# The dense layer's low halves on VectorE instead of GpSimd, in an attention and mixture-of-experts kernel on one core

## The chip, the core and the metric

The kernel runs on one core of a Trainium2 chip. A core has TensorE (matrix products, written PE in the profile, its weight loads PEld), VectorE (DVE), ScalarE (ACT), GpSimd (POOL) and SyncE (SP, which issues DMAs). The metric is the time of one execution on the device in microseconds (us).

## What is computed

The reference has three parts, each feeding the next. Shapes are those of the run.

```python
# q, k, v: (4, 8, 576, 64); attention in blocks of 64 rows, lower-triangular by blocks
attn = softmax(mask(q @ k.T / sqrt(64)));  x = attn @ v        # -> 2304 tokens x 512
# dense layer (the "moe" of the reference)
h = x @ w_in              # 512 -> 2048, float64 weights
g = h - tanh(h)
x = g @ w_out             # 2048 -> 512
# routed layer: 8 experts, top 1, tokens with x @ w_skip <= 0 pass through
e = argmax(x @ w_gate); p = max(softmax(x @ w_gate))
y = x + p * (relu(x @ w1[e]) @ w2[e])
```

## The kernel before

All products run on float32r operands in pairs: a value is split into a high half `hi`, a rounded copy that ScalarE makes, and a low half `lo = value - hi`, and a product is the sum of three matmuls, hi·lo, lo·hi and hi·hi. So each operand that is made on the chip costs one copy on ScalarE and one subtraction on another engine.

The order of every engine's work is the order in which the program is written; nothing is rescheduled. After the attention comes the dense layer, `moe1`. It takes the hidden axis in two halves of 1024. In each half it walks over six groups of 384 tokens, and in each group over eight chunks of 128 hidden values: 96 steps in all, numbered s, 48 in the first half and 48 in the second. A step does this:

- `hidden(s)` (L508): 12 matmuls of 384 columns, into one of three PSUM banks `h`.
- `mm2(s-3)` (L561): 9 matmuls of 512 columns that add the chunk of three steps ago to three PSUM banks `acc`, one for each 128 tokens.
- `act(s)`: g = h - tanh(h) with a polynomial in place of tanh for small h. ScalarE makes u (L533), t (L534) and y (L535), VectorE makes w from h and u (L536), t = h - t (L537), w from y and w (L538). Then `split_g(s-1)` splits the previous step's w into `gh` (ScalarE, L549) and `gl` (L550). Then ScalarE makes the mask k (L541), and VectorE puts t into w where k says so (L542). t, u, y and k have one buffer each, so L534 of the next step waits for L542 of this one.
- `X.split` (L448, L449), in four of each group's eight steps: a quarter of the next group's tokens, `xg`, is split into the pair `xhl`, the high half on ScalarE and the low half in L449.
- `side(s)`: in the first half a decoder turns the float64 weights into pairs. One chunk takes ScalarE's L48, VectorE's L49 to L52, and then ScalarE's L53 and GpSimd's subtraction L54, the last two in the step after. 20 chunks are spread over the 48 steps: one in every second step of the first eight, then two in every five.

When a group's eight steps are summed, `finish` runs from inside `act`, ahead of L541. In the first half it copies the three banks `acc` on ScalarE (L578) and stores them. In the second half VectorE adds the first half's sums (L584), and the rows go through the routing: TensorE turns them (L602, with one PSUM bank for it), ScalarE and VectorE split them (L608, L609), then come logits and small VectorE operations, and GpSimd scatters the records with indirect DMAs (L685).

The routed layer follows: GpSimd gathers tokens (L801), and TensorE runs L834 and L893.

Of the kernel before, what the change touches and what calls it, by code (L numbers as in the profile page):

```python
# [9 lines left out]
F32 = mybir.dt.float32  # L10
# [21 lines left out]
class Decoder:  # L32
    """float64 words -> hi/lo float32r pairs, one chunk of 512 values per partition at a time."""

# [28 lines left out]

class Plan:
    """The order in which the query blocks of a pair of heads go through the attention, and how many
    blocks each stage runs behind the scores."""

# [10 lines left out]
class Banks:  # L78
    """The eight banks of PSUM, three of them for each of two uses and two single ones."""

# [12 lines left out]
def attention(nc, tc, ctx, d, ident, q, k, v, xTd, PS, spare, between, ending, NP=None):  # L93
    """spare: 6144 float32r a partition, used up to the last pair but one"""
    L = ctx.enter_context(tc.tile_pool(name="attl", bufs=2))
# [5 lines left out]
    pt0 = P.tile([128, 2, 4, 128], F32, name="pt0")  # L101
    # blocks 4-8 of the probabilities: four chunks of keys each, and the last block's fifth behind three of zeros
    pts = []
# [51 lines left out]
    def prep_q(n, bank=PS.single):  # L155
        """transposes of q into the two diagonal blocks, scaled"""
        qr, qb = raws[n][1], qbd[n % 2]
        pq, pr = bank(), bank()
        for j in range(4):
            nc.tensor.transpose(pq[:, 128 * j:128 * j + 128], qr[:, j].rearrange("p h d -> p (h d)"), ident)  # L160
        nc.tensor.transpose(pr[:, 0:64], qr[0:64, 4].rearrange("p h d -> p (h d)"), ident[0:64, 0:64])
        yield
        for hh in range(2):
            sl = slice(64 * hh, 64 * hh + 64)
            evac_q(qb[sl, 0:8, sl], pq[sl].rearrange("d (i n) -> d i n", i=8))
            evac_q(qb[sl, NB - 1, sl], pr[sl, 0:64])
        yield
# [76 lines left out]
    def transposes(n, i):  # L244
        """emits the transposes of block i; notes the copies out of PSUM that they allow"""
        nj = i // 2 + 1
# [39 lines left out]
    def pv_early(n):  # L286
        """blocks 0-3 of both heads"""
        vr = vrs.pop(n)
        xp = PS.single()
        for hh in range(2):  # L290
            hs = slice(64 * hh, 64 * hh + 64)
            for j in range(2):
                nc.tensor.matmul(
                    xp[hs, 128 * j:256].rearrange("p (i c) -> p i c", c=64), vr[:, j, hh, :],
                    pt0[:, j, 2 * j:4, hs], start=(j == 0), stop=(j == 1),
                )
        yield
        xs = L.tile([128, 256], F32, tag="xs0", name="xs0", bufs=2)
        evac("xs0", xs, xp[:, 0:256])
        yield  # L300
        b, hp = pairs[n]
        nc.sync.dma_start(out=xTd[hp * 128:hp * 128 + 128, b * d.S:b * d.S + 256], in_=xs)

    def pv_late(n, hh, xs):
        """blocks 4-8 of one head"""
        vv = vhl[n % 2]
# [23 lines left out]
    load(1)  # L330
    # the tensor engine's clock rises while the first rows are on their way
    w = PS("acc")
# [55 lines left out]
NSLOT, MORE = 256, 128  # L388
# the units of routed tokens after the first expert's two: where the ones of MORE tokens stand among those of NSLOT
UNITS = (NSLOT, NSLOT, MORE, NSLOT, MORE, NSLOT, MORE)  # L390
# [5 lines left out]
class Route:  # L396
    """Tables of the routed tokens by expert.

    The first unit is filled by the expert that leads after NEARLY groups, with tokens of all
    groups but the last; the last group's tokens of that expert follow in its next units."""  # L400

# [23 lines left out]
class Tokens:  # L425
    """The attention's rows, transposed, as hi/lo pairs of a group at a time; loaded for each half."""

# [15 lines left out]

    def split(self, u, c, eng=None):
        if u >= 2 * NG:
            return
        xg, x = self.raw.pop((u, c)), self.hl[u]
        self.nc.scalar.copy(x[:, 0, c], xg)  # L448
        (eng or self.nc.gpsimd).tensor_tensor(x[:, 1, c], xg, x[:, 0, c].bitcast(F32), op=ALU.subtract)  # L449


class Consts:
    def __init__(self, nc, pool, d):
# [30 lines left out]
        self.col = index("col", [e, e], [[0, e], [1, e]])  # L484
        # the experts before each one
        self.before = t([128, e, e], F32, name="before")
# [12 lines left out]
def hidden(nc, X, PS, W, hs, s):  # L499
    """chunk s % 8 of a half's hidden axis, for a group of tokens"""  # L500
    u, f = divmod(s, 8)
# [11 lines left out]
def moe1(nc, tc, ctx, X, T, PS, d, C, W, x2p, x2s, tab, out, side, route, hs):  # L513
    """g(x w_in) w_out in two halves of the hidden axis; the second half routes the tokens.

    W[h] = (w_in, w_out) as [128, 2, 4, 1024] and [128, 2, 8, 512] hi/lo pairs.
    side(step) runs other work between the chunks. Returns the last group's routing, to be
    advanced by the caller."""
    P = ctx.enter_context(tc.tile_pool(name="m1", bufs=1))
# [25 lines left out]
    def split_g(s):  # L545
# [3 lines left out]
        nc.scalar.copy(gh, w)  # L549
        nc.gpsimd.tensor_tensor(gl, w, gh.bitcast(F32), op=ALU.subtract)  # L550

# [18 lines left out]
    def finish(u):  # L570
        """the token tiles of a group, once their sums are complete"""
        g = u % NG
# [17 lines left out]
        lp = PS("lp")  # L590
        # in the weights of w_out that are not in use: the other half's, and then this one's
        xh, xl = (
# [60 lines left out]
        nc.scalar.activation(ex, ex, AF.Exp)  # L653
        # the active ones as a factor of the one-hot rows; then what moves the others out of the table
        nc.vector.scalar_tensor_tensor(v, v, 1.0, b8(m2), op0=ALU.mult, op1=ALU.is_equal)
# [96 lines left out]
class Moe2:  # L752
    """The experts' two products over units of 256 or 128 routed tokens."""

# [6 lines left out]
    def load_piece(self, e, j, q=None):  # L761
        """piece j (of 8) of an expert's weights, as it lies in memory; e may be a register"""
        nc = self.nc
# [64 lines left out]
    def mm1(self, x, w, f):  # L828
        """the hidden layer's chunk f, transposed"""
        wi, h = self.W[w][0], self.PS("h")  # L830
# [9 lines left out]
    def mm1_few(self, x, w, z):  # L840
        """chunks 2z and 2z + 1 of the hidden layer of MORE tokens, as rows of tokens"""
        wi, h = self.W[w][0], self.PS("h")
# [76 lines left out]
    def prepare(self, row):  # L919
        """the first unit's tokens, as steps"""  # L920
        self.recs, self.xrs, self.xx = {0: self.load_rec(row, self.nc.sync)}, {}, {}
# [9 lines left out]
    def run(self, sizes, lead, tail, then, units):  # L931
        """units of sizes[k] tokens; the first two are the leading expert's, whose weights are in place.

        tail: the last group's routing, and then() what follows it; units(): (expert, first record)
        of the units from the third on"""
        K = len(sizes)
# [69 lines left out]
    def one(self, e, row):  # L1006
        """a run of MORE tokens on its own"""
        rec = self.load_rec(row, nt=1)
# [21 lines left out]
def entries(nc, pool, d, C, route, out):  # L1030
    """what remains after the leading expert's two units: (expert, first record row) of each entry, and their number.

    The first entries, up to NBIG, are pairs of MORE tokens (the last of a pair may be short), the
    others are runs of up to MORE tokens; entries past the number are empty ones. As steps."""
    E, N = d.E, NENTRY
# [14 lines left out]
    yield  # L1050
    # the pairs, as many as there are big units; the rest in single runs
    v.tensor_tensor(up, up2(pair), C.before, op=ALU.mult)
# [7 lines left out]
    v.memset(st[:, 2 * E:], float(E * d.NT))  # L1060
    # how many entries end with each expert's
    for z in range(2):
# [14 lines left out]
    yield  # L1077
    # the first row: the expert's first one, and so many tokens as the entries of its kind before hold
    v.tensor_tensor(dif, st[:, 1:], st[:, 0:2 * E], op=ALU.subtract)
# [16 lines left out]
def tile_kernel(ctx, tc, q, k, v, moe_w_in, moe_w_out, moe2_w_skip, moe2_w_gate, moe2_w1, moe2_w2, out):  # L1096
# [44 lines left out]
    def decode(z):  # L1141
        """a chunk of the float64 weights: steps, with loads running two chunks ahead"""
        for i in range(2 if z == 0 else 0):
# [7 lines left out]
    with ExitStack() as actx:  # L1151
# [5 lines left out]
        def between(n):  # L1157
# [12 lines left out]
            if n == 3:  # L1170
                # the rows that the first gather covers and no token has filled by then
                zr = ip.tile([128, 1, d.DM], F32, name="zr")
# [9 lines left out]
        def ending(n):  # L1182
            if FIRST_X <= n < FIRST_X + 2:
                X.split(0, 2 * (n - FIRST_X), nc.vector)
                X.split(0, 2 * (n - FIRST_X) + 1, nc.vector)
            if n == -6:
# [101 lines left out]
```

## Time and profile before

| | |
|---|---|
| median of three runs | 906.24 us (905.58 to 907.66) |
| profiled execution, its span | 904.2 us |
| TensorE busy | 845.3 us (93%) |
| VectorE busy | 732.1 us (81%), 1541 instructions |
| ScalarE busy | 567.2 us (63%) |
| GpSimd busy | 404.5 us (45%), 454 instructions |
| chain that ended last | TensorE 38%, VectorE 30%, "issue" 16%, DMA 5%, ScalarE 5%, GpSimd 3% |
| L550 on GpSimd | 96 times, 1029 ns each |
| L449 on GpSimd | 44 times, 1309 ns each |

The profile is of one execution. Busy time of TensorE includes matmuls that overlap, so a busy TensorE is not one at its peak. The chain is followed back from the last instruction to what released each step. "Idle before, releaser" is the time for which an engine stood still and the instruction that ended it.

### The profile page before, as it was taken

The page shows a single profiled execution, that of the slowest core. Times are in us where ns is not written, and L with a number is a line of the kernel's source. Part 1 is how long each engine was busy: PE and PEld are TensorE (multiplying, and loading weights), DVE is VectorE, ACT ScalarE, POOL GpSimd, SP SyncE. Part 2 cuts the span into 40 slices and gives each one's busy share as a digit, 9 for nine tenths or more (in the row PEclk, how much of TensorE's full clock was granted, in tenths as well). Part 3 has the DMA queues.
Part 4 walks back from the last instruction along what each step waited for, and adds up shares of the span by engine and source line. Part 5 has one row for each costly group of instructions (what it writes and reads, how often), then busy time and mean ns, then how long its engine had stood idle before and what let it go on. Part 6 is the DMA issues. An engine that isn't in the chain of part 4 may idle for free.

```text
span 904.2 us, 15078 instructions
## 1 busy us (share of the span) xinstructions
PE 845.3 (93%) x4715; PEld 718.1 (79%) x4715; DVE 732.1 (81%) x1541; ACT 567.2 (63%) x1332; POOL 404.5 (45%) x454
## 2 busy tenths in 40 slices
PE   7999999999987979989898999999999879999996
PEld 5777777776876868879787988878788679999995
DVE  6899999999798888888887778787887725678772
ACT  5888989888556576666656646555576214466651
POOL 5777767777344453534434344444334222124101
PEclk9999999999999989899899999999999999999999
DMA  7365443533213232231403123040252345687860
GB/s 164 85 161 149 106 135 88 145 97 101 79 47 117 65 99 82 70 105 47 134 10 105 71 70 128 13 141 12 90 199 90 110 140 174 203 279 264 279 212 23
DMA packets 102836, 106.06 MB, mean 117 GB/s; under 512 B 64807, under 2 KB 75175, under 8 KB 102754
## 3 DMA queue, kind: packets, MB, share of 16 engines
q1 hardware_dynamic: 99554, 98.52, 36.0%
q0 software_dynamic: 3200, 6.55, 2.2%
q8 instruction: 38, 0.62, 0.3%
q14 instruction: 44, 0.36, 0.1%
HBM read 82.61 MB, written 23.78 MB: 118 GB/s over the span
## 4 chain that ended last, share of the span: by engine, by line
PE 38%; DVE 30%; issue 16%; DMA 5%; ACT 5%; POOL 3%; SPq 1%; DVEq 0%; POOLq 0%; ACTq 0%
DVE w L538 8%; PE acc L561 6%; PE h L200 6%; PE h L508 6%; DVE w L542 5%; PE h L834 5%; PE acc L893 4%; DVE w L536 3%; PE acc L266 2%; DVE word L51 2%; ACT t L534 2%; DVE st L208 2%; DMA xg<-xTd 2%; DMA xr<-x2s,rec 1%; PE lp L316 1%
## 5 line engine op out<-in xcount | busy, mean ns | idle before, releaser
L508 PE MATMUL h<-xhl,wi 128*128 128x384 f32 x1152 | 222.9, 343 | 1.5 <-DVE xhl L449 1.1
L508 PEld LDWEIGHTS h<-xhl,wi 128*128 128x128 f32 x1152 | 207.7, 191 | 10.6 <-DVE xhl L449 1.8
L550 POOL TENSOR_TENSOR gl<-w,gh 128x384 fp32r<-128x384 f32 x96 | 98.7, 1029 | 235.9 <-ACT gh L549 180.8
L561 PE MATMUL acc<-wo,gh 128*128 128x512 f32 x576 | 157.7, 410 | 24.7 <-ACT o L578 20.9
L561 PEld LDWEIGHTS acc<-wo,gh 128*128 128x128 f32 x576 | 108.5, 194 | 46.4 <-ACT o L578 23.6
L240 POOL TENSOR_TENSOR p<-p,st 128x64 f32<-128x64 f32 (+2 forms) x144 | 103.3, 722 | 60.1 <-DVE st L239 27.7
L538 DVE SCALAR_TENSOR_TENSOR w<-y,w 128x384 f32<-128x384 f32 x96 | 127.8, 1331 | 0.0
L200 PE MATMUL h<-kT,qbd 128*128 128x128 f32 (+7 forms) x320 | 106.0, 423 | 4.2 <-ACT p L219 1.6
L536 DVE SCALAR_TENSOR_TENSOR w<-h,u 128x384 f32<-128x384 f32 x96 | 53.2, 554 | 46.8 <-ACT t L534 36.8
L534 ACT ACTIVATE t<-h 128x384 f32<-128x384 f32 x96 | 47.1, 491 | 69.1 <-DVE w L542 68.9
L542 DVE COPY_PREDICATED w<-k,t 128x384 f32<-128x384 int32 x96 | 77.1, 803 | 11.4 <-ACT k L541 2.1
L561 PE MATMUL acc<-wo,gl 128*128 128x512 f32 x288 | 85.6, 407 | 0.1
L834 PE MATMUL h<-xhl,wi 128*128 128x256 f32 x576 | 78.3, 285 | 0.0
L834 PEld LDWEIGHTS h<-xhl,wi 128*128 128x128 f32 x576 | 75.5, 191 | 3.2
L533 ACT ACTIVATE u<-h 128x384 f32<-128x384 f32 x96 | 47.0, 489 | 47.5 <-issue 34.0
L893 PE MATMUL acc<-wo,hp 128*128 128x512 f32 x288 | 74.6, 394 | 0.0
L219 ACT ACTIVATE p<-h,st 128x64 f32<-128x64 f32 (+7 forms) x128 | 65.0, 509 | 7.0 <-DVE st L234 5.4
L908 POOL DMA_INDIRECT out_dram<-o,rec x15 | 16.8, 1117 | 114.8 <-DVE o L905 105.9
L561 PEld LDWEIGHTS acc<-wo,gl 128*128 128x128 f32 x288 | 56.2, 196 | 14.3 <-POOL gl L550 0.5
L208 DVE TENSOR_REDUCE st<-h 128x1 f32<-128x64 f32 (+7 forms) x128 | 56.9, 444 | 9.4 <-PE h L200 8.7
L200 PEld LDWEIGHTS h<-kT,qbd 128*128 128x128 f32 x320 | 50.6, 196 | 15.5 <-ACT p L219 4.5
L449 POOL TENSOR_TENSOR xhl<-xg,xhl 128x384 fp32r<-128x384 f32 x44 | 57.6, 1309 | 8.2 <-ACT xhl L448 8.2
(234 smaller groups left out, 1627.5 us busy)
## 6 DMA issues: line engine op xcount, KB each, us to landing
stage<-in_moe_w_dram SPq DMA_DIRECT2D x64, 512.0 KB, 4.4
xg<-xTd SPq DMA_DIRECT2D x48, 192.0 KB, 2.8
stage<-in_moe_w_in_dram SPq DMA_DIRECT2D x16, 512.0 KB, 4.1
stage<-in_moe_w_out_dram SPq DMA_DIRECT2D x16, 512.0 KB, 3.3
x2p<-o SPq DMA_DIRECT2D x18, 256.0 KB, 3.3
part<-x2p SPq DMA_DIRECT2D x18, 256.0 KB, 3.2
out_dram<-part SPq DMA_DIRECT2D x18, 256.0 KB, 2.5
x2s<-part SPq DMA_DIRECT2D x18, 256.0 KB, 2.7
```

The source lines that it names most:

```text
L200: nc.tensor.matmul(s[:, 0:z - a], qb[:, i, :], kT[:, a:z], start=True, stop=True)
L208: nc.vector.reduce_max(nm, ss[0][:, 0:nk], axis=AX.X, negate=True)
L240: nc.gpsimd.tensor_tensor(prob[i][:, 0:nk], prob[i][:, 0:nk], ri.to_broadcast([128, nk]), op=ALU.mult)
L508: nc.tensor.matmul(h[:, 0:TG], w[:, a, c, fs], x[:, b, c], start=(n == 0), stop=(n == 11))
L534: nc.scalar.activation(t, h, AF.Tanh)
L536: nc.vector.scalar_tensor_tensor(w, h, POLY_C2, u, op0=ALU.mult, op1=ALU.mult)
L538: nc.vector.scalar_tensor_tensor(w, y, POLY_K, w, op0=ALU.add, op1=ALU.mult)
L542: nc.vector.copy_predicated(w, k.bitcast(I32), t)
L550: nc.gpsimd.tensor_tensor(gl, w, gh.bitcast(F32), op=ALU.subtract)
L561: nc.tensor.matmul(accs[u][t], g[a][:, t * 128:t * 128 + 128], w[:, b, f], start=(f == 0 and b == 1), stop=(f == NF - 1 and a == 1),)
L834: self.nc.tensor.matmul(h[:, 0:NSLOT], wi[:, a, c, f * 128:f * 128 + 128], x[:, b, c], start=(n == 0), stop=(n == 11))
L893: nc.tensor.matmul(acc[t], hp[:, a, t * 128:t * 128 + 128], wo[:, b, f], start=(f == 0 and b == 1), stop=(f == 7 and a == 1),)
```

## The change

Both low halves of the dense layer, of the activations (`gl`, L550) and of the tokens (`xhl`, L449), are subtracted on VectorE. The subtraction keeps its place in the program text; the engine's name is what differs. The decoder's L54 stays on GpSimd. The four splits of the first group, which named VectorE before, are as they were. Line numbers are the same in both kernels.

```diff
-    def split(self, u, c, eng=None):
+    def split(self, u, c):
         if u >= 2 * NG:
             return
         xg, x = self.raw.pop((u, c)), self.hl[u]
         self.nc.scalar.copy(x[:, 0, c], xg)
-        (eng or self.nc.gpsimd).tensor_tensor(x[:, 1, c], xg, x[:, 0, c].bitcast(F32), op=ALU.subtract)
+        self.nc.vector.tensor_tensor(x[:, 1, c], xg, x[:, 0, c].bitcast(F32), op=ALU.subtract)
...
         gh, gl, w = gs[s]
         nc.scalar.copy(gh, w)
-        nc.gpsimd.tensor_tensor(gl, w, gh.bitcast(F32), op=ALU.subtract)
+        nc.vector.tensor_tensor(gl, w, gh.bitcast(F32), op=ALU.subtract)
```

VectorE in the first half of the dense layer, two steps with a decoder's chunk between them, before:

```order
L538 SCALAR_TENSOR_TENSOR w<-y,w 128x384
L542 COPY_PREDICATED w<-k,t 128x384
L49 TENSOR_SCALAR word<-word 128x512
L50 TENSOR_SCALAR word<-word 128x512
L51 SCALAR_TENSOR_TENSOR word<-stage,word 128x512
L52 SCALAR_TENSOR_TENSOR word<-stage,word 128x512
L536 SCALAR_TENSOR_TENSOR w<-h,u 128x384
L537 TENSOR_TENSOR t<-h,t 128x384
L538 SCALAR_TENSOR_TENSOR w<-y,w 128x384
L542 COPY_PREDICATED w<-k,t 128x384
```

and the same place after:

```order
L542 COPY_PREDICATED w<-k,t 128x384
L449 TENSOR_TENSOR xhl<-xg,xhl 128x384
L49 TENSOR_SCALAR word<-word 128x512
L50 TENSOR_SCALAR word<-word 128x512
L51 SCALAR_TENSOR_TENSOR word<-stage,word 128x512
L52 SCALAR_TENSOR_TENSOR word<-stage,word 128x512
L536 SCALAR_TENSOR_TENSOR w<-h,u 128x384
L537 TENSOR_TENSOR t<-h,t 128x384
L538 SCALAR_TENSOR_TENSOR w<-y,w 128x384
L550 TENSOR_TENSOR gl<-w,gh 128x384
L542 COPY_PREDICATED w<-k,t 128x384
```

L550 now stands between L538 and L542 of every step, and L449 behind L542 in four steps of a group.

VectorE in the second half, between the first and the second split of the routed rows (L609), before:

```order
L609 TENSOR_TENSOR wo_108<-tp,wo_108 128x4x128
L536 SCALAR_TENSOR_TENSOR w<-h,u 128x384
L537 TENSOR_TENSOR t<-h,t 128x384
L538 SCALAR_TENSOR_TENSOR w<-y,w 128x384
L542 COPY_PREDICATED w<-k,t 128x384
L609 TENSOR_TENSOR wo_108<-tp,wo_108 128x4x128 x2
```

and after:

```order
L609 TENSOR_TENSOR wo_108<-tp,wo_108 128x4x128
L536 SCALAR_TENSOR_TENSOR w<-h,u 128x384
L537 TENSOR_TENSOR t<-h,t 128x384
L538 SCALAR_TENSOR_TENSOR w<-y,w 128x384
L550 TENSOR_TENSOR gl<-w,gh 128x384
L542 COPY_PREDICATED w<-k,t 128x384
L449 TENSOR_TENSOR xhl<-xg,xhl 128x384
L609 TENSOR_TENSOR wo_108<-tp,wo_108 128x4x128 x2
```

Two more subtractions stand ahead of the second L609. GpSimd, from the last attention work to the first scatters, before (its first rows):

```order
L54 TENSOR_TENSOR wo_108<-word,wo_108 128x512
L240 TENSOR_TENSOR p_146<-p_146,st 128x320
L550 TENSOR_TENSOR gl<-w,gh 128x384
L449 TENSOR_TENSOR xhl<-xg,xhl 128x384
L54 TENSOR_TENSOR wo_108<-word,wo_108 128x512
L550 TENSOR_TENSOR gl<-w,gh 128x384
L449 TENSOR_TENSOR xhl<-xg,xhl 128x384
```

and after, where the whole dense layer leaves it the decoder's subtractions and the DMAs:

```order
L240 TENSOR_TENSOR p_146<-p_146,st 128x320
L54 TENSOR_TENSOR wo_108<-word,wo_108 128x512 x4
L54 TENSOR_TENSOR wi_3398<-word,wi_3398 128x512 x8
L54 TENSOR_TENSOR wo_3399<-word,wo_3399 128x512 x8
L685 DMA tab<-rec,pi 20736x2 x15
L801 DMA xr<-x2s,rec_8074 128x512 x2
```

The orders of TensorE, ScalarE and SyncE are the same in both kernels.

## Rows read from the trace of the kernel before

**Rows 1.** Busy time of each engine in two stretches: first half, four groups of second.

```profile
240.14:480.14 240.00, 215.00 (x1011) 190.03 (x1010) 212.18 (x275) 153.51 (x324) 108.72 (x95) 0.94 0.24 78
503.10:658.43 155.33, 150.28 (x802) 130.48 (x801) 123.96 (x244) 86.79 (x192) 66.18 (x60) 1.00 0.25 82
```

**Rows 2.** The chain that ended last, from 240 to 480 us, shares by line.

```profile
by line: DVE w L538 25.3%; issue 18.4%; DVE w L542 15.0%; DVE w L536 9.6%; DVE word L51 5.3%; ACT t L534 5.2%; DVE word L50 3.3%; PE acc L561 2.6%; DVE word L49 2.6%; DMA xg<-xTd 2.5%; PE h L508 2.0%; ACT o L578 1.8%; DVE t L537 1.0%; ACT y
```

**Rows 3.** TensorE's waits for `acc`: the page's group, then one in the timeline.

```profile
L561 PE MATMUL acc<-wo,gh 128*128 128x512 f32 x576 | 157.7, 410 | 24.7 <-ACT o L578 20.9
...
323.72 1.56 ACT L578 COPY o<-acc 128x512 f32<-128x512 f32 x3
...
324.36 1.22 PE L561 MATMUL acc<-wo,gh 128*128 128x512 f32 x2 [5.60 <-ACT o L578]
```

**Rows 4.** Timeline (start, duration): TensorE, two steps following each other, second half.

```profile
547.97 2.28 PE L508 MATMUL h<-xhl,wi 128*128 128x384 f32 x12
...
552.17 2.28 PE L508 MATMUL h<-xhl,wi 128*128 128x384 f32 x12
```

**Rows 5.** Timeline: VectorE in the dense layer's first step, GpSimd idle until 239.32.

```profile
235.57 0.56 DVE L536 SCALAR_TENSOR_TENSOR w<-h,u 128x384 f32<-128x384 f32 x1 [0.47 <-ACT t L534]
236.05 0.55 DVE L537 TENSOR_TENSOR t<-h,t 128x384 f32<-128x384 f32 x1
236.51 0.55 DVE L538 SCALAR_TENSOR_TENSOR w<-y,w 128x384 f32<-128x384 f32 x1
237.16 0.60 DVE L542 COPY_PREDICATED w<-k,t 128x384 f32<-128x384 int32 x1
237.66 0.41 DVE L49 TENSOR_SCALAR word<-word 128x512 f32<-128x512 f32 x1
...
239.90 0.55 DVE L536 SCALAR_TENSOR_TENSOR w<-h,u 128x384 f32<-128x384 f32 x1
```

**Rows 6.** Lines 538, 542 and 449 on VectorE: ns minimum/median/maximum, first and last start.

```profile
L538 DVE SCALAR_TENSOR_TENSOR w<-y,w x96: 541/1373/1699, 236.5 to 697.0; 128x384 f32<-128x384 f32 x96
...
L542 DVE COPY_PREDICATED w<-k,t x96: 585/604/1511, 237.2 to 697.7; 128x384 f32<-128x384 int32 x96
...
L449 DVE TENSOR_TENSOR xhl<-xg,xhl x4: 532/808/1444, 225.3 to 227.7; 128x384 fp32r<-128x384 f32 x4
```

**Rows 7.** Timeline: L538 beside GpSimd's subtraction, then beside its indirect DMA.

```profile
418.64 1.29 POOL L54 TENSOR_TENSOR wo<-word,wo 128x512 fp32r<-128x512 f32 x1 [1.28 <-ACT wo L53]
418.77 1.58 DVE L538 SCALAR_TENSOR_TENSOR w<-y,w 128x384 f32<-128x384 f32 x1
...
421.10 0.49 ACT L534 ACTIVATE t<-h 128x384 f32<-128x384 f32 x1 [2.11 <-DVE w L542]
...
421.69 0.56 DVE L536 SCALAR_TENSOR_TENSOR w<-h,u 128x384 f32<-128x384 f32 x1 [0.63 <-ACT t L534]
...
573.85 0.99 POOL L685 DMA_INDIRECT tab<-rec,pi  x1 [2.36 <-DVE pi L683]
...
574.43 0.55 DVE L538 SCALAR_TENSOR_TENSOR w<-y,w 128x384 f32<-128x384 f32 x1
```

**Rows 8.** Timeline: a routing step of the second half, up to TensorE's wait.

```profile
557.50 1.02 POOL L550 TENSOR_TENSOR gl<-w,gh 128x384 fp32r<-128x384 f32 x1 [2.95 <-ACT gh L549]
557.55 1.38 DVE L538 SCALAR_TENSOR_TENSOR w<-y,w 128x384 f32<-128x384 f32 x1
...
558.48 1.32 POOL L449 TENSOR_TENSOR xhl<-xg,xhl 128x384 fp32r<-128x384 f32 x1
...
560.14 0.67 DVE L609 TENSOR_TENSOR wo<-tp,wo 128x512 fp32r<-128x512 f32 x1
...
560.87 0.66 PE L602 MATMUL tp<-ident,part 128*128 128x128 f32 x4 [1.23 <-DVE wo L609]
```

**Rows 9.** Timeline: the last steps, L550 queued on GpSimd behind the scatters.

```profile
695.00 1.99 POOL L550 TENSOR_TENSOR gl<-w,gh 128x384 fp32r<-128x384 f32 x2
...
696.07 0.56 DVE L536 SCALAR_TENSOR_TENSOR w<-h,u 128x384 f32<-128x384 f32 x1 [1.93 <-POOL gl L550]
```

More of the change, by code (lines that the diff above doesn't have):

```diff
@@ L1183, in ending @@
             if FIRST_X <= n < FIRST_X + 2:
-                X.split(0, 2 * (n - FIRST_X), nc.vector)
-                X.split(0, 2 * (n - FIRST_X) + 1, nc.vector)
+                X.split(0, 2 * (n - FIRST_X))
+                X.split(0, 2 * (n - FIRST_X) + 1)
             if n == -6:
```

## The prediction

> **What bounds the kernel now.** I first read the busy times by stretch. The dense layer's first half takes 240.0 us for 48 steps, 5.00 us each, from the first `mm2` to the resumption of `mm2` in the second half. VectorE is busy for 212.18 us of it, TensorE runs at 0.94 of its clock, and in the second half's four groups it is at 1.00 [rows 1]. Then the chain of the first half: L538, L542 and L536, all VectorE, hold half of it, and TensorE's lines under 5% [rows 2]. So the first half goes at VectorE's pace. TensorE runs up to three steps ahead, until the next group's first `mm2` needs `acc`, whose copies sit on ScalarE behind `t` and so behind L542. Of 24.7 us that L561 waits ahead of `gh` matmuls, 20.9 us end with L578 [rows 3]; there are six such waits, one a group, 2.5 to 5.6 us long.
>
> What is TensorE's own pace? In undisturbed steps `hidden` starts 552.17 - 547.97 = 4.20 us apart [rows 4], 48 x 4.20 = 201.6 us. The first half is thus 38.4 us above TensorE's floor, 24.7 us of waits and the rest the lower clock that follows them. The second half is already at the floor, but for its routing.
>
> Why is VectorE slow? Its subtractions and L538 read two operands from SBUF, as GpSimd's do. L538 takes 1373 ns in the median and 541 ns at the least [rows 6]. In the row where GpSimd has just begun a 1.29 us subtraction it takes 1.58 us and ends 0.42 us after it; beside an indirect DMA, which keeps GpSimd busy but is no subtraction, it takes 0.55 us [rows 7]. L537, which reads PSUM, never stretches. So VectorE waits out GpSimd's subtraction nearly whole: moving `gl` takes from VectorE a wait as long as the operation that it is given.
>
> **The change, step by step.** I write a step from the start T of L536, with starts taken from the one step with GpSimd idle [rows 5]: L537 at T + 0.48, L538 at T + 0.94, and L542 0.65 later because it waits for L538's result; what follows L542 comes 0.50 later.
>
> (a) L550 on VectorE. Its nearest row is L449, the same shape on VectorE: 532 ns alone, 1444 ns beside GpSimd [rows 6]; the price in time is between 0.46 us, the distance between two independent operations [rows 5], and 1.44 us. I take 0.47 us, since GpSimd has only 20 subtractions left here. It fits in the space where L542 waited for L538: L550 at T + 1.41, L542 at T + 1.88, done at T + 2.48. So it adds 0.94 - 0.65 = 0.29 us. Its operand `gh` follows y on ScalarE and is there before L538 ends, so it makes no new wait; L542 is what is queued behind it, and `mm2(s-3)` needs it only two steps later. The buffer that it writes was released by a `mm2` that TensorE runs before the `hidden` of this step.
>
> (b) L538 falls from 1.37 to 0.55 us, 0.82 us in each of the steps where GpSimd met it.
>
> (c) L449 on VectorE, four a group, stands behind L542. ScalarE's copy is done by then. In a plain step VectorE next waits for L534, which needs L542's end, 0.02 us, and has L536 start 0.59 us after it [rows 7]; L449 ends within this wait, and costs nothing. If a decoder's chunk follows instead, it costs 0.50 us. L542 loses its encounters with GpSimd's L449 (median 604 ns, longest 1511 ns [rows 6]).
>
> So a plain step takes 2.48 + 0.02 + 0.59 = 3.09 us. A step with a decoder's chunk takes T + 2.38 for the start of L49 and 239.90 - 237.66 = 2.24 us for the four operations [rows 5], 4.62 us, and 4.87 us with half an L449 on average. The step behind it meets the decoder's L54, still on GpSimd, as L538 does in [rows 7]: 1.58 in place of 0.55 us, so 4.12 us. Five steps hold two chunks: 2 x 4.87 + 2 x 4.12 + 3.09 = 21.07 us, against TensorE's 5 x 4.20 = 21.0 us. VectorE and TensorE come out level.
>
> On top, once a group, the three copies of `acc` (1.56 us [rows 3]) stand before L541 on ScalarE and hold L542 back by about 1.0 us. A group of eight steps then needs 8 x 4.21 + 1.0 = 34.7 us of VectorE and 33.6 us of TensorE. Two engines that are level don't interlock without loss, since chunks come unevenly; I take 35.0 us a group. Six groups: 210.0 us, against 240.0 before. **30.0 us** gained in the first half, and the clock should stay at 1.00, as it does in the second half, where TensorE waits little [rows 1].
>
> (d) Second half. Plain steps stay at 4.20 us; VectorE's 3.09 us lie beside TensorE. In a routing step the second L609 starts at 560.14, and TensorE waits 1.23 us for it [rows 8]. After, from L538 at 557.55: L550 0.47, L542 0.94, L449 1.44, L609 1.93 us later, at 559.48. This is 0.66 us earlier, with two more operations ahead of it. Five groups show this wait: **3.3 us**, between nothing and 5 x 1.23 = 6.2 us.
>
> (e) Last steps. On GpSimd L550 stands behind three indirect DMAs, and VectorE waits 1.93 us for it [rows 9]; TensorE is hardly held. The gathers of the routed layer stand behind the last L550. I take **1.0 us**, between 0 and 2.
>
> Sum: 30.0 + 3.3 + 1.0 = 34.3 us off the profiled execution's 904.2 us gives 869.9 us. The median of the runs is 2.0 us above this execution, so **872 us**.
>
> A rule that speaks against the change: the Trainium skill, "Vector Engine (DVE) Microarchitecture Reference", section "Points that are easy to get wrong", says that a scalar-tensor-tensor with two SBUF sources that aren't bf16 runs at half throughput. By it L538 would be long by itself. The 0.55 us rows don't bear it out, and the third rival says what it would cost.
>
> **The rivals.**
>
> *TensorE's floor.* If L54 meets VectorE less than I count (in its idle time for `t`, or in L536 and L537, which read PSUM), VectorE has slack, TensorE never waits, and the first half is 201.6 us: 38.4 us gained, and up to 6.2 and 2 more. That is 860 to 864 us, 862 us as its value. For it: VectorE without L54 needs 21.07 - 2 x 1.03 = 19.0 us for five steps. Against it: L54 follows L52 at a fixed distance, as in [rows 7], so it should hit each time.
>
> *VectorE still ahead.* If unevenness leaves TensorE the shortest wait of today, 2.5 us a group, and half a microsecond of the clock's cost, a group takes 33.6 + 2.5 + 0.5 = 36.6 us, the first half 219.6 us. 20.4 us gained and nothing in the second half: 883.8 + 2.0 = 886 us.
>
> *Slower.* If L538 is long by its own reading of SBUF, moving L550 takes nothing away and VectorE just gets more: 8 x 0.29 + 2 x 0.50 = 3.3 us a group, 20 us in the first half, and in five routing steps 0.29 + 0.50 = 0.8 us more wait, 4 us. That is 930 us. It decides if L538 stays near 1.37 us with GpSimd idle. For it speaks that most L538 are long; against it the short ones, whose neighbour is no subtraction.
>
> *No change.* GpSimd's 96 + 44 subtractions leave it and VectorE gets them, so that the edit does nothing is excluded. The time could still stand if another wait took its place: ScalarE is busy for 153.51 of 240 us [rows 1] and doesn't bind, so I see only a cancellation of the two effects.
>
> **How the numbers follow.** My forecast, level engines, 872 us: 0.51. TensorE's floor, 862 us: 0.23. VectorE still ahead, 886 us: 0.19. No change: 0.02. Slower, 930 us: 0.05. The range reaches from the floor, 860 us, to the second rival's 886 us; a part of each lies beyond the ends, so it holds about 8 in 10. A measurement of this kernel tells 0.2% (1.8 us) from no change. Faster by more: 0.51 + 0.23 + 0.19 = 0.93, within: 0.02, slower: 0.05.
>
> **What would show it.** L538's median near 550 ns, with about 20 long ones in the first half beside L54; L550 on VectorE near 550 ns; the waits that end with L578 under 6 us in sum; TensorE's clock at 1.00 from 284 us on; the first half (48 steps from 240 us) at 210 us; the wait ahead of L602 near 0.6 us. Wrong would be a long L538 with GpSimd idle, or waits of L561 of 2 us and more that stay.

## The result, and the profile after

The changed kernel takes 869.5 us in the median of four runs (867.64 to 872.83), against 906.59 us for the kernel before; the ratio is 0.9612, with a 95% interval of 0.958 to 0.9645. The profiled execution has a span of 868.6 us, 35.6 us less than before.

Where the 35.6 us come from, by the starts of matmuls in TensorE's timeline (the first `mm2` of either half, the first L834):

| stretch | before | after | change |
|---|---|---|---|
| up to the first `mm2` | 240.3 | 242.0 | +1.7 |
| first half of the dense layer, 48 steps | 239.8 | 208.9 | -31.0 |
| second half, to the routed layer's first product | 230.9 | 223.0 | -7.9 |
| routed layer | 193.2 | 194.7 | +1.5 |

No instruction of the first and the last line was changed. What differs there is TensorE's granted clock: in the profile after, it stood at its lower level (0.5, which is 1.2 GHz) for 3.4 us from 228.7 us on, where it was at 1.00 before, and early in the routed layer for 6.8 us, where the profile before has 3.4 us. The first half of the dense layer is nearly the whole result. The busy times by stretch, in the columns of [rows 1], for this half and for four groups of the second:

```profile
241.96:450.82 208.86, 203.93 (x1010) 181.64 (x1009) 193.58 (x350) 153.44 (x326) 26.56 (x20) 1.00 0.28 90
472.38:623.58 151.20, 149.29 (x801) 130.53 (x800) 113.50 (x293) 86.09 (x192) 12.65 (x12) 1.00 0.26 82
```

In the first half VectorE runs 350 instructions in place of 275 and is busy for less time, 193.6 against 212.2 us. GpSimd falls from 108.7 to 26.6 us, its 20 decoder's subtractions. TensorE is busy for 203.9 of 208.9 us, and its clock is at 1.00, where [rows 1] has 0.94. The chain from 240 to 440 us, answering to [rows 2], now leads with TensorE:

```profile
by line: PE acc L561 16.9%; PE h L508 16.8%; issue 12.9%; DVE w L538 11.3%; DVE w L542 7.5%; ACT y L535 4.1%; DVE word L51 3.9%; DVE word L52 3.8%; DVE w L536 3.2%; ACT gh L549 2.7%; DVE word L50 2.4%; ACT o L578 2.2%; ACT t L534 1.9%; DVE 
```

The lines of the page for L561 (busy, mean ns, idle before and its releaser), answering to [rows 3]:

```profile
L561 PE MATMUL acc<-wo,gh 128*128 128x512 f32 x576 | 151.0, 397 | 2.9 <-ACT o L578 2.9
...
L561 PE MATMUL acc<-wo,gl 128*128 128x512 f32 x288 | 83.1, 397 | 2.0 <-DVE gl L550 2.0
```

The waits for the copies of `acc` have fallen from 20.9 to 2.9 us. The wait in the second line is new: TensorE waits 2.0 us in all for `gl`, where it was 0.1 us before.

Durations by line on VectorE (minimum/median/maximum in ns), answering to [rows 6]:

```profile
L538 DVE SCALAR_TENSOR_TENSOR w<-y,w x96: 537/549/1665, 238.2 to 659.5; 128x384 f32<-128x384 f32 x96
...
L550 DVE TENSOR_TENSOR gl<-w,gh x96: 542/551/555, 244.0 to 662.0; 128x384 fp32r<-128x384 f32 x96
...
L542 DVE COPY_PREDICATED w<-k,t x96: 580/598/615, 238.8 to 660.4; 128x384 f32<-128x384 int32 x96
```

L538's median has gone from 1373 to 549 ns, and L542's longest case from 1511 to 615 ns. L550 never takes over 555 ns. The long cases of L538 that are left stand beside L54, as in this piece of the timeline:

```profile
409.20 1.30 POOL L54 TENSOR_TENSOR wo<-word,wo 128x512 fp32r<-128x512 f32 x1 [10.42 <-ACT wo L53]
409.31 1.59 DVE L538 SCALAR_TENSOR_TENSOR w<-y,w 128x384 f32<-128x384 f32 x1
```

And the routing step that [rows 8] shows, after: the five operations of VectorE start 0.46 to 0.49 us apart, none of them stretched, and TensorE waits 0.47 us where it waited 1.23 us.

```profile
525.47 0.54 DVE L538 SCALAR_TENSOR_TENSOR w<-y,w 128x384 f32<-128x384 f32 x1
525.93 0.54 DVE L550 TENSOR_TENSOR gl<-w,gh 128x384 fp32r<-128x384 f32 x1
526.40 0.59 DVE L542 COPY_PREDICATED w<-k,t 128x384 f32<-128x384 int32 x1
526.89 0.53 DVE L449 TENSOR_TENSOR xhl<-xg,xhl 128x384 fp32r<-128x384 f32 x1
527.35 0.67 DVE L609 TENSOR_TENSOR wo<-tp,wo 128x512 fp32r<-128x512 f32 x1
...
528.08 0.66 PE L602 MATMUL tp<-ident,part 128*128 128x128 f32 x4 [0.47 <-DVE wo L609]
```

### The profile page after: what moved, and what is told of

Same layout as the page of the kernel before. It is cut to its first block, busy times and chain, and to the rows that moved or that the text cites. A ratio compares the mean times of both kernels' runs of the same rounds, so it can differ in the third digit from the quotient of the medians.

```text
span 868.6 us, 14970 instructions
## 1 busy us (share of the span) xinstructions
PE 832.7 (96%) x4715; PEld 710.9 (82%) x4715; DVE 698.7 (80%) x1681; ACT 565.6 (65%) x1332; POOL 249.3 (29%) x314
## 4 chain that ended last, share of the span: by engine, by line
PE 35%; issue 34%; DVE 17%; ACT 5%; DMA 3%; POOL 3%; SPq 1%; POOLq 0%; DVEq 0%; ACTq 0%
PE h L200 6%; PE h L834 6%; PE acc L893 5%; PE h L508 4%; PE acc L561 4%; DVE w L538 3%; PE acc L266 2%; DVE st L208 2%; DVE w L542 2%; DVE word L51 2%; DVE word L52 1%; DMA xr<-x2s,rec 1%; PE lp L316 1%; PE tp L316 1%; POOL tab L685 1%
## 5 line engine op out<-in xcount | busy, mean ns | idle before, releaser
L508 PE MATMUL h<-xhl,wi 128*128 128x384 f32 x1152 | 220.4, 340 | 1.1 <-DVE xhl L449 1.1
L561 PE MATMUL acc<-wo,gh 128*128 128x512 f32 x576 | 151.0, 397 | 2.9 <-ACT o L578 2.9
L561 PEld LDWEIGHTS acc<-wo,gh 128*128 128x128 f32 x576 | 105.3, 188 | 21.9 <-ACT o L578 5.0
L536 DVE SCALAR_TENSOR_TENSOR w<-h,u 128x384 f32<-128x384 f32 x96 | 53.3, 555 | 46.4 <-ACT t L534 38.9
L561 PE MATMUL acc<-wo,gl 128*128 128x512 f32 x288 | 83.1, 397 | 2.0 <-DVE gl L550 2.0
L685 POOL DMA_INDIRECT tab<-rec,pi x18 | 20.2, 1124 | 212.4 <-DVE pi L683 198.9
L834 PE MATMUL h<-xhl,wi 128*128 128x256 f32 x576 | 78.7, 286 | 0.0
L834 PEld LDWEIGHTS h<-xhl,wi 128*128 128x128 f32 x576 | 76.0, 192 | 3.2
L538 DVE SCALAR_TENSOR_TENSOR w<-y,w 128x384 f32<-128x384 f32 x96 | 71.6, 746 | 0.0
L561 PEld LDWEIGHTS acc<-wo,gl 128*128 128x128 f32 x288 | 53.8, 188 | 16.3 <-DVE gl L550 3.7
L881 ACT ACTIVATE hp<-h 128x256 fp32r<-128x256 f32 x48 | 18.4, 384 | 65.1 <-PE h L834 61.2
L542 DVE COPY_PREDICATED w<-k,t 128x384 f32<-128x384 int32 x96 | 57.3, 597 | 3.8 <-ACT k L541 3.7
L541 ACT ACTIVATE k<-u,bias 128x384 f32<-128x384 f32 x96 | 60.0, 625 | 0.0
```

Of the source, the lines that this page charges most:

```text
L508: nc.tensor.matmul(h[:, 0:TG], w[:, a, c, fs], x[:, b, c], start=(n == 0), stop=(n == 11))
L536: nc.vector.scalar_tensor_tensor(w, h, POLY_C2, u, op0=ALU.mult, op1=ALU.mult)
L538: nc.vector.scalar_tensor_tensor(w, y, POLY_K, w, op0=ALU.add, op1=ALU.mult)
L541: nc.scalar.activation(k, u, AF.Relu, bias=C.bias[:, 1:2])
L542: nc.vector.copy_predicated(w, k.bitcast(I32), t)
L561: nc.tensor.matmul(accs[u][t], g[a][:, t * 128:t * 128 + 128], w[:, b, f], start=(f == 0 and b == 1), stop=(f == NF - 1 and a == 1),)
```

## The experiments

The theory is that VectorE's operations with two operands in SBUF wait while GpSimd subtracts, because both engines want the same way into SBUF (a port). Rival A says that ports have no part in it: VectorE makes `gl` in half of GpSimd's time, so `mm2` gets it earlier. Eight kernels tell them apart; each is compared with the kernel before on the same chip, which took 905.82 or 905.57 us there, where it took 906.59 us beside the changed kernel.

**One half of the change alone.** First only `gl`:

```diff
-        nc.gpsimd.tensor_tensor(gl, w, gh.bitcast(F32), op=ALU.subtract)
+        nc.vector.tensor_tensor(gl, w, gh.bitcast(F32), op=ALU.subtract)
```

> Only gl (L550) moves to VectorE, the token halves (L449) stay on GpSimd. Theory (VectorE waits out GpSimd's subtractions that read SBUF): L538 falls to about 550 ns as in the changed kernel, but L542 still meets L449 in four steps of a group, about 0.65 us each; some 8 to 10 us in the first half and 1 to 2 us in the routing steps more than the changed kernel: 878 to 882 us. Rival A (gl simply comes earlier to mm2, since VectorE makes it in half GpSimd's time, and no port is involved): all of the gain is in gl, so 870 us.

Measured: 874.13 us, ratio 0.9628 (0.9599 to 0.9657). It lies between the two expectations, and 4 us under mine. L538's median is 548 ns, as expected. But L542 hardly suffers from L449 on GpSimd: its median is 597 ns, and two of its 96 cases take over 0.9 us. In 26 of its 44 cases GpSimd's L449 starts while L550 is running on VectorE, and there GpSimd takes longer: L449 takes 1386 ns in the median and 1004 at the least. (It was long in the kernel before too, 1330 ns, mostly behind L538.) By stretches, the first half takes 215.5 us, 6.6 us more than in the changed kernel, where 8 to 10 were expected. The second half takes 220.9 us, 2.1 us less, where 1 to 2 us more were expected: without L449 ahead of the second L609, TensorE doesn't wait for it in the first four groups.

Then only the token halves (L449), with `gl` on GpSimd:

```diff
-        (eng or self.nc.gpsimd).tensor_tensor(x[:, 1, c], xg, x[:, 0, c].bitcast(F32), op=ALU.subtract)
+        (eng or self.nc.vector).tensor_tensor(x[:, 1, c], xg, x[:, 0, c].bitcast(F32), op=ALU.subtract)
```

> Only the token halves (L449) move to VectorE, gl stays on GpSimd. Theory: L538 keeps its median of 1.37 us, L542 loses its long cases of 1.2 us in four steps of a group; 895 to 903 us. Rival A: the token halves have slack, so no change, 906 us.

Measured: 894.0 us, ratio 0.9847 (0.9816 to 0.9878), 1 us under the band that I gave. L538 stays at a median of 1368 ns. Rival A, which gave 906 us, doesn't hold for this half: nobody waited long for the token halves, yet taking them from GpSimd brought 11.8 us. The parts give 31.7 and 11.8 us, together more than the 37 us of both. By stretches, they give 24.3 and 9.8 us in the first half, where both give 31.0, and 10.0 and 3.0 us in the second, where both give 7.9. In the first half there are only 38 us between VectorE's pace and TensorE's, and both parts draw on them. In the second half, moving L449 gains 3.0 us while `gl` is on GpSimd, and costs 2.1 us once `gl` has left it.

**GpSimd keeps everything, and L538 reads PSUM.** Here GpSimd subtracts as before; only one operand of L538 moves out of SBUF:

```diff
-        nc.vector.scalar_tensor_tensor(w, h, POLY_C2, u, op0=ALU.mult, op1=ALU.mult)
         nc.vector.tensor_tensor(t, h, t, op=ALU.subtract)
-        nc.vector.scalar_tensor_tensor(w, y, POLY_K, w, op0=ALU.add, op1=ALU.mult)
+        nc.vector.scalar_tensor_tensor(h, h, POLY_C2, u, op0=ALU.mult, op1=ALU.mult)
+        nc.vector.scalar_tensor_tensor(w, y, POLY_K, h, op0=ALU.add, op1=ALU.mult)
```

> GpSimd keeps every subtraction as before; instead the first product of w is written over h in PSUM (after t has read h), so that L538 reads one operand from SBUF and one from PSUM. Theory: L538 falls to about 600 ns though GpSimd subtracts beside it; L542 still meets GpSimd; 876 to 888 us. Rival A: nothing is changed for gl, 906 us. Rival B (L538 is long because of a conflict with GpSimd whatever it reads): 906 us, L538 still near 1.37 us.

Measured: 868.81 us, ratio 0.9574 (0.9545 to 0.9602). This is all of the change's gain, with no subtraction moved, and 7 us under the band that I gave: L542, which I expected to go on meeting GpSimd, takes over 0.9 us in 10 of its 96 cases, where it was 30 before. The lines' durations (L538 and `gl` on GpSimd), and one step of the timeline:

```profile
L538 DVE SCALAR_TENSOR_TENSOR w<-y,h x96: 553/554/556, 238.4 to 659.6; 128x384 f32<-128x384 f32 x96
...
L550 POOL TENSOR_TENSOR gl<-w,gh x96: 1004/1021/1544, 241.2 to 661.7; 128x384 fp32r<-128x384 f32 x96
```

```profile
423.53 1.02 POOL L550 TENSOR_TENSOR gl<-w,gh 128x384 fp32r<-128x384 f32 x1 [1.96 <-ACT gh L549]
...
423.74 0.56 DVE L538 SCALAR_TENSOR_TENSOR w<-y,h 128x384 f32<-128x384 f32 x1
```

L538 runs in the middle of GpSimd's subtraction and takes 0.56 us; over all 96 the longest is 556 ns. Rival A falls here, as `gl` is made by the same engine in the same 1021 ns. So does a conflict whatever L538 reads. It is the second source in SBUF that makes L538 wait.

The control has the new order of the three lines, with w in SBUF:

```diff
-        nc.vector.scalar_tensor_tensor(w, h, POLY_C2, u, op0=ALU.mult, op1=ALU.mult)
         nc.vector.tensor_tensor(t, h, t, op=ALU.subtract)
+        nc.vector.scalar_tensor_tensor(w, h, POLY_C2, u, op0=ALU.mult, op1=ALU.mult)
```

> Control for the run before: t is subtracted ahead of the first product of w, and w stays in SBUF. All theories: within 4 us of 906 us, L538 with a median near 1.37 us.

Measured: 908.60 us, ratio 1.0026 (1.0008 to 1.0045). L538's median is 1254 ns, a little less than expected, but it isn't the order that helps.

**The wait put back, by a result that nobody reads.** The changed kernel, and GpSimd subtracts once more into a tile that nobody reads:

```diff
         nc.vector.tensor_tensor(gl, w, gh.bitcast(F32), op=ALU.subtract)
+        idle = P.tile([128, TG], BF16, tag="idle", name="idle")
+        nc.gpsimd.tensor_tensor(idle, w, gh.bitcast(F32), op=ALU.subtract)
```

> The changed kernel, and GpSimd also subtracts gh from w in every step into a tile that nobody reads (in bf16), when gh is there, as it did before. Theory (a subtraction on GpSimd makes VectorE's two-operand reads from SBUF wait): the wait comes back though nothing depends on GpSimd's result; L538 or L550 long again in nearly every step, five steps of VectorE 21.1 + 5 x 0.82 = 25.2 us, first half some 240 us, 900 to 912 us in all. Rival A (gl earlier for mm2): nobody waits for the new operation, so 870 us.

Measured: 911.09 us, ratio 1.007 (1.0046 to 1.0093). One idle operation a step takes back 41.6 us, more than the whole gain. The first half takes 237.8 us, against 208.9 in the changed kernel and 239.8 before. (In the second half a part of the price has another cause: four times, 6.2 us in all, L536 waits for the idle operation to give the buffer of w free. The first half has no such wait.) A step of its timeline:

```profile
301.71 1.43 POOL L552 TENSOR_TENSOR idle<-w,gh 128x384 bf16<-128x384 f32 x1 [2.95 <-ACT gh L549]
301.71 0.55 DVE L538 SCALAR_TENSOR_TENSOR w<-y,w 128x384 f32<-128x384 f32 x1
...
302.18 1.38 DVE L550 TENSOR_TENSOR gl<-w,gh 128x384 fp32r<-128x384 f32 x1
```

The two engines start together at 301.71. L538 gets through in 0.55 us, GpSimd takes 1.43 us in place of 1.02 us, and then L550 waits until GpSimd is done at 303.14 and ends 0.42 us after it. So which of the operations is long depends on who comes first, and the later one waits for the other.

The same with a GpSimd operation that reads one operand:

```diff
+        nc.gpsimd.tensor_scalar(idle, gh.bitcast(F32), 1.0, 1.0, op0=ALU.mult, op1=ALU.mult)
```

> As the run before, but GpSimd's extra operation reads one operand from SBUF (gh times one times one) instead of two, at the same place. Theory as I have it (GpSimd holds VectorE off for as long as it reads SBUF): L538 or L550 longer by the operation's own duration less 0.2 us, 880 to 912 us. Rival C (only two-operand reads of GpSimd collide with those of VectorE): L538 and L550 stay at 550 ns, 870 us.

Measured: 879.69 us, ratio 0.9728 (0.9698 to 0.9758), 10 us slower than the changed kernel; just under the band that I gave. The two lines that meet, and one step of the timeline:

```profile
L550 DVE TENSOR_TENSOR gl<-w,gh x96: 545/859/1643, 243.0 to 672.7; 128x384 fp32r<-128x384 f32 x96
...
L552 POOL TENSOR_SCALAR idle<-gh x96: 510/829/1012, 240.0 to 672.4; 128x384 bf16<-128x384 f32 x96
```

```profile
299.78 0.55 DVE L538 SCALAR_TENSOR_TENSOR w<-y,w 128x384 f32<-128x384 f32 x1
299.87 0.83 POOL L552 TENSOR_SCALAR idle<-gh 128x384 bf16<-128x384 f32 x1 [2.50 <-ACT gh L549]
...
300.25 0.86 DVE L550 TENSOR_TENSOR gl<-w,gh 128x384 fp32r<-128x384 f32 x1
```

GpSimd's operation takes 510 ns at the least. Here it comes just after L538, takes 0.83 us, and L550 ends 0.41 us after it; L550's median grows from 551 to 859 ns. Rival C, by which one operand wouldn't collide, falls. With the shorter operation the price is smaller too: 0.31 us for L550, against 0.82 us with the subtraction.

**What is left: the decoder's L54.** The changed kernel with L54 of the 20 chunks of the dense layer on VectorE as well:

```diff
-    def steps(self, raw, hi, lo):
+    def steps(self, raw, hi, lo, eng):
...
-        yield nc.gpsimd.tensor_tensor(lo, xf, hi.bitcast(F32), op=ALU.subtract)
+        yield eng.tensor_tensor(lo, xf, hi.bitcast(F32), op=ALU.subtract)
...
-        for i, _ in enumerate(dec.steps(words.pop(z), dst(0), dst(1))):
+        for i, _ in enumerate(dec.steps(words.pop(z), dst(0), dst(1), nc.gpsimd if z < AHEAD else nc.vector)):
```

> The changed kernel with the decoder's last subtraction (L54) on VectorE too, for the 20 chunks of the dense layer. Theory: each L54 costs VectorE about 1.03 us of waiting from GpSimd and about 0.6 us if it does it itself; five steps 21.1 - 2 x 0.4 = 20.2 us, under TensorE's 21.0; no long L538; waits for acc near nothing; 862 to 869 us. Rival TensorE-bound already: 869 us, no change.

Measured: 864.46 us, ratio 0.9544 (0.9515 to 0.9572), within the band, and 5 us faster than the changed kernel. Its first half, from the first `mm2`, and the page's line for the waits:

```profile
243.25:446.45 203.20, 202.63 (x1009) 182.31 (x1009) 183.92 (x371) 153.01 (x327) 0.00 (x0) 1.00 0.29 93
```

```profile
L561 PE MATMUL acc<-wo,gh 128*128 128x512 f32 x576 | 150.7, 397 | 0.5 <-ACT o L578 0.5
```

VectorE runs 20 subtractions of 0.68 us more and is busy for 9.7 us less, since no operation is long any more: L538, L550, L542 and L449 have 20 cases over 900 ns in the changed kernel's dense layer, and none here. 48 steps take 203.2 us, against the floor of 201.6 us, and the waits for `acc` are 0.5 us. This is the fastest kernel of this study.

Last, both ways of sparing L538 at once, the change and the product over h in PSUM, with L54 on GpSimd:

> The changed kernel and the product over h in PSUM together, L54 on GpSimd. Theory: L54 can't stretch L538 any more, only L550 or L542 now and then; VectorE needs 19 to 21 us for five steps; near TensorE's floor, 862 to 869 us. If the two edits act on the same wait they don't add: not faster than 862 us.

Measured: 868.37 us, ratio 0.9597 (0.9569 to 0.9625). It is at the upper end of the band and no better than the change alone. The collisions with L54 have moved and become shorter: 18 of the 20 long cases are now L550, as here, 0.93 us in place of 0.55, where L538 took 1.58. A step that meets L54 takes 3.60 us in the median, against 4.06.

```profile
251.23 0.93 DVE L550 TENSOR_TENSOR gl<-w,gh 128x384 fp32r<-128x384 f32 x1
```

Against this stands a longer plain step. The product over h is now made just ahead of L538, which waits for it and starts 1.13 us after L536, where it was 0.94 us; a plain step takes 3.22 us in place of 3.04. The first half is 207.4 us, 1.4 us shorter than with the change alone, and in the second half TensorE's wait ahead of L602 grows from 0.47 to 0.84 us.

## Why the prediction was right, step by step

The forecast was 872 us, 34.3 us off the profiled execution; measured are 869.5 us and 35.6 us. The mechanism held. That the sum came so near is luck in part: the loss that is left in the first half lies in other places than it said, and the second half gave 3.6 us more than forecast, most of it through the clock.

**What bounds it, and the wait that goes.** VectorE set the first half's pace by waiting for GpSimd's subtractions; the run with w in PSUM shows that it is the operand in SBUF that makes L538 wait, and the idle subtraction that nothing else is needed to bring the first half's time back. The prediction named L538 and L542. The decoder's L52, which reads two operands from SBUF as well, waited too: in the kernel before, 19 of its 20 cases in the dense layer take over 0.9 us (1545 ns in the median), and none in the changed kernel (691 ns). The sum isn't hurt by it, since it took its price for a chunk from a step with GpSimd idle. The rule that was weighed against the change, half throughput for a scalar-tensor-tensor with two SBUF sources (the Trainium skill, "Vector Engine (DVE) Microarchitecture Reference", section "Points that are easy to get wrong"), isn't borne out: L538 takes 549 ns with its sources in SBUF and 554 ns with one in PSUM. Another page of the Trainium skill, "SBUF — State Buffer", section "SBUF: two separate sides", says that the ports which VectorE and GpSimd share are held by whichever starts first for a whole instruction; the trace agrees, with L550 ending 0.42 us after the idle subtraction, and in the other direction, where only `gl` has moved, with GpSimd's L449 at 1386 in place of 1004 ns.

**(a) to (c), the first half.** Forecast 30.0 us, measured 31.0: 208.9 us for 48 steps where 210.0 was said. VectorE's steps are as they were worked out. The starts of L536, one a step, in the changed kernel's timeline of VectorE (rows between them left out):

```profile
327.25 0.56 DVE L536 SCALAR_TENSOR_TENSOR w<-h,u 128x384 f32<-128x384 f32 x1
...
331.86 0.55 DVE L536 SCALAR_TENSOR_TENSOR w<-h,u 128x384 f32<-128x384 f32 x1
...
335.92 0.56 DVE L536 SCALAR_TENSOR_TENSOR w<-h,u 128x384 f32<-128x384 f32 x1 [0.56 <-ACT t L534]
...
338.96 0.56 DVE L536 SCALAR_TENSOR_TENSOR w<-h,u 128x384 f32<-128x384 f32 x1 [0.56 <-ACT t L534]
```

The first step holds a decoder's chunk and no L449: 4.61 us, worked out 4.62. The second meets L54: 4.06 us, worked out 4.12. The third is plain: 3.04 us, worked out 3.09. The signs came too: 18 long cases of L538 (and two of L449) for the 20 L54, 2.9 us of waits for `acc` where under 6 were expected, and a clock of 1.00.

But the sum had VectorE and TensorE level throughout, at 35.0 us a group, and that isn't what the runs show. From `mm2` to `mm2` the six groups take 38.2, 35.3, 33.8, 33.7, 34.1 and 33.8 us. In the last four TensorE runs within 0.5 us of its floor of 33.6 us, as the first rival had it; of the 7.3 us that the half stands above its floor, 6.3 us lie in the first two groups. So 8.4 us above the floor were forecast and 7.3 measured, in other places. The run with L54 moved fits this: the first half is 5.7 us shorter, 4.9 us of it in the first two groups, and stands 1.6 us above the floor. Why VectorE falls behind in the first two groups and not later, no run shows by itself.

**One step of (a) was wrong.** It said that L550 makes no new wait. At the dense layer's start there is one: the first `mm2` follows its three `hidden` at once, and L550 stands behind an L538 that waits out L54, so TensorE waits 1.07 us. With two more of 0.46 us, at 253.7 and 262.9 us, that is the new wait of 2.0 us for `gl`, all of it in the first group. With `gl` on GpSimd and w in PSUM it is 0.0, and so it is with L54 moved:

```profile
L561 PE MATMUL acc<-wo,gl 128*128 128x512 f32 x288 | 83.0, 396 | 0.0
```

**(d) and (e), the second half.** Forecast 3.3 us for five waits ahead of L602, and 1.0 us for the last steps; the stretch gave 7.9 us. The waits came out as forecast in sum, 5.6 us before and 2.4 us after. But only four of the five were 1.23 us, and these fell to 0.47 to 0.49 us; the fifth was 0.67 us and fell by 0.2 us.

The rest is mostly the clock. The first five steps of the second half gave 1.4 us by the two windows below: TensorE ran at 0.93 of its clock there before and at 1.00 after (22.96 and 21.56 us for the same work), a leftover of the first half's last wait that the sum hadn't counted.

```profile
480.14:503.10 22.96, 22.96 (x107) 20.45 (x108) 17.36 (x22) 14.06 (x32) 9.19 (x9) 0.93 0.29 95
```

```profile
450.82:472.38 21.56, 21.56 (x109) 19.48 (x109) 14.34 (x29) 12.95 (x29) 0.00 (x0) 1.00 0.30 97
```

The last group and what follows it up to the first L834 gave 2.2 us in place of 1.0. Only 0.5 us of it come before its last `mm2` ends, 0.2 us of it the fifth wait's; before, one of the weight loads there waited for an L550 behind the scatters:

```profile
696.09 0.53 PEld L561 LDWEIGHTS acc<-wo,gl 128*128 128x128 f32 x3 [0.54 <-POOL gl L550]
```

The other 1.7 us lie behind it: before, the clock stood at 0.5 for 3.4 us from 706.4 us on, and the eight matmuls of L615 took 2.72 us; after, it was at 1.00 and they took 1.62 us. So (e) gave less than half of its 1.0 us, and the clock, which no term held, gave more than the rest. Of a middle group's 0.96 us the wait explains 0.76 us; the other 0.2 us stay open.

**The rivals.** TensorE's floor, 862 us, was named with the reason against it, that L54 hits at a fixed distance: in the profiled kernel it does, 20 times of 20, and taking L54 away gives 864.5 us. In the last four groups of the first half TensorE stood near this floor all the same. "VectorE still ahead" doesn't show: of the 24.7 us that L561 waited ahead of `gh` matmuls, 2.9 us are left. "Slower" hung on L538 being long by itself; it isn't.

## What to carry to other kernels

Before work is left to GpSimd because VectorE is full, look for the shortest and the median duration of VectorE's operations with two SBUF operands: if they differ by most of GpSimd's operation (here 0.83 us of 1.02), each such operation costs VectorE more as a wait than as work (here 0.82 us against 0.29 us). There are two ways out that gave the same here, to move the subtraction to VectorE, or to let one source of the operation that waits lie in PSUM. Where VectorE's queue stands ahead of a wait of TensorE, an operation more on it costs time: in the second half, L449 was 2.1 us better on GpSimd once `gl` had left it. If a wait has gone, look for who is level next, stretch by stretch; here the last 1.03 us collisions were worth 5 us, and then TensorE bounds.

## What the runs showed of the hardware

Which side pays isn't fixed. With both on SBUF, an operation of VectorE that begins with GpSimd's or ahead of it takes 0.55 us and GpSimd's grows (1.43 us in place of 1.02); an L538 or L550 that begins later ends about 0.42 us after GpSimd's. So, with only `gl` moved, L449 mostly waits for L550 and L542 stays short. And neither operation need have two inputs in SBUF. On GpSimd's side, one with a single SBUF operand held L550 up to a median of 859 ns, while the indirect DMA of [rows 7] left L538 at 0.55 us. On VectorE's side, the decoder's L49 reads one operand from SBUF: with only `gl` moved it takes over 0.9 us in 8 of its 20 cases in the dense layer, up to 1205 ns, and each of these ends 0.28 to 0.29 us after GpSimd's L449; in the kernel before its median there is 412 ns.
